# A mixture of experts on one core: quarter-row gathers issued one per unit of work instead of two

## The chip, the cores and the metric

The kernel runs on one core of a Trainium2 chip. The metric is device time in microseconds (us) of one execution, lower is better. The core has five engines that run at once, each with its own list of instructions in program order: TensorE (PE, matrix products), VectorE (DVE), ScalarE (ACT), GpSimd (POOL) and SyncE (SP, which here issues plain transfers). They wait for each other by semaphores.

## The reference

Attention for 8 batches of 8 heads (576 positions, head size 64) gives 4608 token rows of 512 numbers; then each token goes through one expert of eight, the one that its gate picks.

```python
logits = x @ w_gate                       # x: 4608 x 512, the attention's output
e_idx = np.argmax(logits, axis=1)
...
for e in range(E):                        # E = 8 experts, hidden size 1024
    mask = e_idx == e
    h = np.maximum(x[mask] @ w1[e], 0.0)
    ye = h @ w2[e]
    out[mask] = gate_w[mask, None] * eom[mask, e, None] * ye
```

## The kernel before

**Two phases.** The attention fills the first half of the time and stores each token's row (with its factors, 640 numbers) in DRAM as `xd`. The experts' phase works through 21 *slots*. A slot is up to 256 tokens of one expert ("pair"), or up to 128 ("single"); three pairs take up to 64 more tokens (three "long" slots, 9, 14 and 18). Slots 0 to 4 are pairs whose tokens are all known before the attention ends, and they gather whole rows. Slots 5 to 20 are the rest: 7, 10, 13, 16 and 19 are singles, the others pairs.

**A slot is eight units**, `j` = 0 to 7, written by `slot(s)`. Units 0 to 3 make the hidden layer: `first` puts 24 matmuls of a pair (12 of a single) into a PSUM tile `ph`, ACT takes the rectified result (`ht`, line 1417; 1400 in long slots), DVE the rest of it (line 1418 or 1401). There are two `ph` buffers, so the product of unit j+2 waits until ACT and DVE have emptied that of unit j. A single needs a further transpose on PE (`across`). Units 4 to 7 multiply by the second weights into `py` (line 1446). In each unit, ACT and DVE also split the weights of six units ahead into `wh` and `wl` (lines 1302, 1304; in singles, POOL makes two of eight `wl`), and SP loads those of eight units ahead. At unit 7 ACT and DVE write `y`, and POOL scatters it to `out` (line 1458; two or three scatters for a pair, one for a single).

**Gathers.** The rows of a later slot are fetched by POOL as indirect DMAs of 128 quarter rows each (line 1257, `part`): 8 for a pair, 4 for a single, 2 more for a long slot (`xgm`). They land in one of two buffers, `xg` of slot s modulo 2, so those of slot i can start once slot i-2 has been transposed out of it (`xr`, line 1320, and `gs`, line 1332, both on DVE). `gathers(s, j)` runs at the end of each unit: at unit 0 it puts the gathers of the next slots in the list `due`, and then issues up to a fixed number of them. All this only sets the *order* of POOL's list: POOL has no notion of a unit, and goes through gathers back to back until one of its instructions has to wait, which is a scatter (for `y`), a `wl` of a single's weights (for ACT's `wh`) or a gather into a buffer still in use. Where DVE transposes a slot's rows also follows from this bookkeeping: `turns` places the two transposes at units 6 and 7 of the slot two before, if the last gather was issued more than two units ago, and otherwise at units 2 and 3 of the slot before.

Of the kernel before, what the change touches and what calls it, by code (L numbers as in the profile page):

```python
# [870 lines left out]
class Moe:  # L871
# [390 lines left out]
    def gathers(self, s, j):  # L1262

        if j == 6 and s + 2 < self.end and self.whole(s + 2):
            self.gather(s + 2)
        if j == 0:
            for i in range(max(self.asked + 1, s + 2), min(s + 4, self.end)):
                if not self.whole(i):
                    self.due += [(i, b) for b in range(self.blocks(i))]
                    self.asked = i  # L1270
        for _ in range(2):
            if self.due:
                i, b = self.due[0]
                if (self.todo[i][1] if b < 8 else 3) in self.quarters and i - 2 in self.gss_made:
                    self.part(i, b)
                    self.due.pop(0)
                    if not any(g == i for g, _ in self.due):
                        self.asked_at[i] = 8 * s + j
# [329 lines left out]
```

## Time and profile before

| | us |
|---|---|
| median of 3 runs (lowest, highest) | 960.4 (959.22, 962.1) |
| the profiled execution: its own time | 968.01 |
| its span, first to last instruction | 966.2 |
| PE busy in the span | 899.8 (93%) |
| DVE busy | 769.8 (80%) |
| ACT busy | 640.3 (66%) |
| POOL busy | 621.3 (64%) |

The times of lines below are us from the start of the span of that one execution. "Busy" on PE counts its matmuls as the profile models them. An indirect DMA on POOL is shown for as long as POOL prepares it, not until its data lands.

### The profile page before, as it was taken

Reading aid. Unit: us, or ns where it says so; the run is one execution under the profiler, and the core shown is the slowest. Engines: PE = TensorE matmul, PEld = TensorE weight load, DVE = VectorE, ACT = ScalarE, POOL = GpSimd, SP = SyncE. Lnnn points to the kernel's source line nnn. Section 1 sums busy time; section 2 is a strip of 40 time slices with the busy share of each in tenths; the row PEclk is TensorE's granted clock in tenths of the full one; section 3 lists DMA queues with packets and bytes.
Section 4 is the critical chain, followed back from the end, with each engine's and each line's share of the span. In section 5 each row is a group of like instructions: output and inputs, shape, how many; then the busy total and the mean of one; then the engine's idle time right before and its main releaser. Section 6 shows DMA issues by size and latency. Waiting matters only on the chain.

```text
span 966.2 us, 33919 instructions
## 1 busy us (share of the span) xinstructions
PE 899.8 (93%) x14174; PEld 773.8 (80%) x14174; DVE 769.8 (80%) x1498; ACT 640.3 (66%) x1358; POOL 621.3 (64%) x560
## 2 busy tenths in 40 slices
PE   4999999999999999999999986999999998899997
PEld 3777777877878878887898975878979887788986
DVE  6899999999999999999597864859657587378661
ACT  4777788898989989886754533446537465265561
POOL 5788899898989899996221152678646664375310
PEclk9999999999999999999999997999999999999999
DMA  6365675665647565545699763768757677579530
GB/s 237 105 198 196 193 234 179 213 200 187 228 154 253 179 229 179 188 156 167 235 347 300 247 202 115 226 187 329 259 172 264 221 242 236 161 236 304 176 125 22
DMA packets 58624, 200.05 MB, mean 207 GB/s; under 512 B 8996, under 2 KB 11102, under 8 KB 58464
## 3 DMA queue, kind: packets, MB, share of 16 engines
q1 hardware_dynamic: 47616, 175.39, 55.1%
q0 software_dynamic: 9568, 21.27, 6.5%
q8 instruction: 113, 1.85, 0.8%
q10 hardware_dynamic: 1280, 1.15, 0.4%
q14 instruction: 47, 0.39, 0.1%
HBM read 177.21 MB, written 22.43 MB: 207 GB/s over the span
## 4 chain that ended last, share of the span: by engine, by line
PE 24%; issue 15%; POOL 7%; DVE 3%; another core or an unknown queue 2%; DMA 2%; ACT 1%; POOLq 0%; DVEq 0%; ACTq 0%
PE ph L1391 11%; PE py L1446 9%; POOL xg L1257 5%; DMA xg<-xd,1qi 2%; PE acc L612 1%; POOL out L1458 1%; DVE wl L1304 1%; POOL wl L1304 1%; PE py L1451 1%; PE ph L1377 1%; ACT wh L1302 1%; PE sc L566 0%; DVE pm L575 0%; DVE xr L1320 0%
## 5 line engine op out<-in xcount | busy, mean ns | idle before, releaser
L582 ACT ACTIVATE pm<-pm,m 128x576 f32<-128x576 f32 x288 | 222.0, 771 | 49.6 <-DVE pm L575 45.5
L1304 DVE TENSOR_TENSOR wl<-wr,wh 128x1024 fp32r<-128x1024 f32 x158 | 201.5, 1285 | 32.5 <-ACT wh L1302 25.6
L1391 PE MATMUL ph<-xt,wh 128*128 128x256 f32 (+1 forms) x1024 | 199.6, 293 | 24.2 <-issue 13.2
L575 DVE TENSOR_SCALAR_CACHE_REDUCE pm<-sc 128x576 f32<-128x576 f32 x288 | 205.3, 745 | 20.8 <-PE sc L566 14.4
L612 PE MATMUL acc<-pt,v 32*64 32x128 f32 (+1 forms) x9216 | 198.1, 295 | 13.8 <-DVE xb L641 7.7
L1446 PE MATMUL py<-wh,ht 128*128 128x512 f32 x592 | 194.3, 397 | 0.3 <-issue 0.2
L612 PEld LDWEIGHTS acc<-pt,v 32*64 32x64 f32 x9216 | 157.9, 131 | 39.1 <-issue 23.0
L1391 PEld LDWEIGHTS ph<-xt,wh 128*128 128x128 f32 x1024 | 165.0, 193 | 30.0 <-issue 15.6
L566 PE MATMUL sc<-kq 64*128 64x288 f32 x1536 | 162.3, 321 | 16.8 <-ACT kq L527 9.8
L1302 ACT CAST wh<-wr 128x1024 fp32r<-128x1024 f32 x168 | 171.4, 1049 | 0.0
L517 POOL TENSOR_TENSOR raw<-raw,rt 128x1152 f32<-128x1152 f32 x62 | 164.7, 2657 | 6.0 <-DMA raw<-in_qk 6.0
L566 PEld LDWEIGHTS sc<-kq 64*128 64x128 f32 x1536 | 122.8, 190 | 51.2 <-issue 21.2
L1391 PE MATMUL ph<-xt,wl 128*128 128x256 f32 (+1 forms) x512 | 149.4, 292 | 0.5 <-issue 0.5
L1257 POOL DMA_INDIRECT xg<-xd,2qi x88 | 104.9, 1192 | 45.5 <-issue 23.3
L1446 PEld LDWEIGHTS py<-wh,ht 128*128 128x128 f32 x592 | 111.3, 188 | 25.2 <-issue 1.1
L588 DVE STREAM_TRANSPOSE pt<-pm 128x576 f32<-128x576 f32 x160 | 116.7, 759 | 1.2 <-ACT pm L582 1.2
L1446 PE MATMUL py<-wl,ht 128*128 128x512 f32 x296 | 116.4, 393 | 0.7 <-issue 0.7
L1417 ACT ACTIVATE ht<-ph 128x512 fp32r<-128x512 f32 x52 | 31.1, 598 | 109.1 <-PE ph L1391 60.7
L1391 PEld LDWEIGHTS ph<-xt,wl 128*128 128x128 f32 x512 | 98.8, 193 | 0.9 <-issue 0.9
L1418 DVE SCALAR_TENSOR_TENSOR ht<-ph,ht 128x512 fp32r<-128x512 f32 x52 | 35.9, 690 | 70.9 <-ACT ht L1417 43.5
L590 DVE STREAM_TRANSPOSE pt<-pm 128x1152 f32<-128x1152 f32 x64 | 87.9, 1374 | 0.0
L530 POOL TENSOR_TENSOR kq<-raw,kq 128x1152 fp32r<-128x1152 f32 (+1 forms) x33 | 82.7, 2506 | 6.6 <-ACT kq L527 6.6
(308 smaller groups left out, 1159.7 us busy)
## 6 DMA issues: line engine op xcount, KB each, us to landing
wr<-in_w SPq DMA_DIRECT2D x168, 512.0 KB
raw<-in_qk SPq DMA_DIRECT2D x64, 576.0 KB
v<-in_v SPq DMA_DIRECT2D x64, 576.0 KB
xd<-xb SPq DMA_DIRECT2D x16, 640.0 KB
xg<-xd,2qi POOLq DMA_INDIRECT x88
xd<-xb SPq DMA_DIRECT2D x8, 160.0 KB
rt<-in_rope ACTq DMA_DIRECT2D x1, 576.0 KB
out<-y,2idx POOLq DMA_INDIRECT x22
```

The costliest lines, as they stand in the source:

```text
L517: self.eng(eng).tensor_tensor(out=rv, in0=rv, in1=rt, op=ALU.mult)
L566: self.sent.count(2, self.nc.tensor.matmul(self.ps[i][:, a, :HS], st, self.kq[r, mov, x], start=(n == 0), stop=(n == 2)))
L575: self.nc.vector.tensor_scalar(self.halves(i), self.ps[i][:, :, :HS], 1.0, FAR, op0=ALU.mult, op1=ALU.min, accum_out=self.m[i])
L582: self.nc.scalar.activation(self.pc[i], self.pc[i], AF.Exp, bias=self.m[i], scale=-1.0, accum_out=self.z[:, zi:zi + 1])
L588: self.nc.vector.transpose(out=self.pt[:, c + 5 * h, :], in_=self.pc[units[0]])
L590: self.nc.vector.transpose(out=self.pt[:, c:c + 6:5, :], in_=self.pc[units])
L612: m = nc.tensor.matmul(self.acc[h * D:h * D + D, a, o:o + 32 * n], self.v[r, h, j, :], self.pt[r, u:u + n, 32 * j:32 * j + 32], start=(j = ...
L1257: self.nc.gpsimd.indirect_dma_start(out=self.xgs[s % 2][:, b, :] if b < 8 else self.xgm[:, s % 2, b - 8, :], out_offset=None, in_=self.xd. ...
L1302: self.nc.scalar.copy(wh, r)
L1304: eng.tensor_tensor(out=wl, in0=r, in1=wh.bitcast(F32), op=ALU.subtract)
L1391: nc.tensor.matmul(out, st[:, dc, fs], mv[:, dc, 0:N], start=(n == 0), stop=(n == 11))
L1446: self.nc.tensor.matmul(py[h], st[:, f, hs], mv, start=(f == 0 and n == 0), stop=(f == 7 and n == 2))
```

## The change

In each unit, `gathers` issues one gather instead of up to two. It still issues two when the first one due is for the next slot (s+1) or earlier, or for a slot not above `n0` = 5, the first slot that is fetched by quarter rows.

```diff
-        for _ in range(2):
+        for _ in range(2 if self.due and self.due[0][0] <= max(s + 1, self.n0) else 1):
             if self.due:
                 i, b = self.due[0]
                 if (self.todo[i][1] if b < 8 else 3) in self.quarters and i - 2 in self.gss_made:
                     self.part(i, b)
                     self.due.pop(0)
```

No instruction is added or removed. On POOL the same gathers stand at other places between the scatters (`out`) and the `wl`. The first place is from the scatters of slot 5 to those of slot 8; before:

```order
L1458 DMA out_0<-y5_11634,2idx_10882 4608x512 x2
L1257 DMA xg_9170<-xd_83,2qi_10886 128x160 x6
L1304 TENSOR_TENSOR wl57_11799<-wr57_11724,wh57_11798 128x1024
L1257 DMA xg_9170<-xd_83,2qi_10886 128x160 x2
L1257 DMA xgm_11334<-xd_83,3qi_11608 128x160 x2
L1304 TENSOR_TENSOR wl61_11891<-wr61_11856,wh61_11890 128x1024
L1458 DMA out_0<-y6_11903,2idx_10882 4608x512 x2
L1257 DMA xg_9170<-xd_83,1qi_11281 128x160 x4
L1458 DMA out_0<-y7_12109,1idx_11277 4608x512
L1257 DMA xg_9170<-xd_83,2qi_10886 128x160 x8
L1458 DMA out_0<-y8_12370,2idx_10882 4608x512 x2
L1257 DMA xg_9170<-xd_83,2qi_10886 128x160 x6
```

and of the change, on the same engine and between the same scatters:

```order
L1458 DMA out_0<-y5_11619,2idx_10882 4608x512 x2
L1257 DMA xg_9170<-xd_83,2qi_10886 128x160 x4
L1304 TENSOR_TENSOR wl57_11778<-wr57_11709,wh57_11777 128x1024
L1257 DMA xg_9170<-xd_83,2qi_10886 128x160 x4
L1304 TENSOR_TENSOR wl61_11870<-wr61_11829,wh61_11869 128x1024
L1458 DMA out_0<-y6_11882,2idx_10882 4608x512 x2
L1257 DMA xg_9170<-xd_83,2qi_10886 128x160 x5
L1257 DMA xgm_11325<-xd_83,3qi_11593 128x160 x2
L1257 DMA xg_9170<-xd_83,1qi_11275 128x160
L1458 DMA out_0<-y7_12085,1idx_11271 4608x512
L1257 DMA xg_9170<-xd_83,1qi_11275 128x160 x3
L1257 DMA xg_9170<-xd_83,2qi_10886 128x160 x4
```

Behind a pair's scatters stand four gathers instead of six (slots 5 and 8), behind those of slot 6, where the single slot 7 begins, eight instead of four. The same pattern repeats for slots 8 to 17.

The second place is the start of POOL's quarter-row work. Before the scatters of slot 4 (`out` from y4) stood two gathers of slot 6, a gather of a list (`1tk`) and six more; in the change five follow `1tk`, and the rest goes behind the scatters:

```order
-L1257 DMA xg<-xd,2qi 128x160 x2
+L1257 DMA xg<-xd,2qi 128x160
 L955 DMA 1tk<-lst_85,1ri 11x128
-L1257 DMA xg<-xd,2qi 128x160 x6
-L1458 DMA out<-y_11311,0idx 4608x512 x2
-L1257 DMA xg<-xd,1qi 128x160 x2
+L1257 DMA xg<-xd,2qi 128x160 x5
+L1458 DMA out<-y_11305,0idx 4608x512 x2
+L1257 DMA xg<-xd,2qi 128x160
```

Two gathers of slot 6 have moved behind slot 4's scatters.

On DVE one thing moves: the transposes of slot 9 (`xr9`) and its factors (`gs9`), which stood before the first hidden part of slot 8 (`ht1_8`), now stand around the last one. Of the change:

```order
L1418 SCALAR_TENSOR_TENSOR ht1_8_12094<-ph8_2_12176,ht0_8_12093 128x512
L1304 TENSOR_TENSOR wl72_12204<-wr72_12135,wh72_12203 128x1024
L1320 STREAM_TRANSPOSE xr9_0_12209<-xg_9170 128x4x4x32
L1418 SCALAR_TENSOR_TENSOR ht1_8_12094<-ph8_3_12211,ht0_8_12093 128x512
L1304 TENSOR_TENSOR wl73_12239<-wr73_12171,wh73_12238 128x1024
L1320 STREAM_TRANSPOSE xr9_1_12244<-xg_9170 128x4x4x32
```

The lists of PE, ACT and SP are the same as before.

## Rows read from the trace of the kernel before

**Rows 1.** Stretches: length, busy PE, PEld, DVE, ACT, POOL; granted clock, DMA share, GB/s.

```profile
480.00:562.00 82.00, 81.71 (x523) 72.97 (x522) 69.18 (x183) 43.48 (x60) 13.68 (x12) 1.00 0.88 297
562.00:600.00 38.00, 26.01 (x140) 22.79 (x139) 16.72 (x39) 11.76 (x16) 19.78 (x20) 0.78 0.48 139
600.00:870.00 270.00, 256.69 (x1546) 228.59 (x1545) 187.17 (x290) 142.54 (x205) 161.24 (x124) 0.99 0.71 231
870.00:966.00 96.00, 89.61 (x541) 80.25 (x539) 56.58 (x79) 44.85 (x65) 26.34 (x20) 0.98 0.47 156
```

**Rows 2.** PE's time line: the matmuls before which it sat idle.

```profile
575.73 0.50 PE L1391 MATMUL ph<-xt,wh 128*128 128x256 f32 x2 [3.09 <-issue]
...
590.79 0.80 PE L1391 MATMUL ph<-xt,wh 128*128 128x256 f32 x2 [4.38 <-DVE ht L1418]
...
639.23 0.51 PE L1391 MATMUL ph<-xt,wh 128*128 128x256 f32 x2 [1.09 <-DVE ht L1418]
...
704.45 0.56 PE L1391 MATMUL ph<-xt,wh 128*128 128x320 f32 x2 [2.35 <-DVE ht L1401]
...
770.39 0.50 PE L1391 MATMUL ph<-xt,wh 128*128 128x256 f32 x2 [1.79 <-issue]
...
803.98 0.41 PE L1391 MATMUL ph<-xt,wh 128*128 128x320 f32 x1 [0.98 <-DVE ht L1401]
...
812.08 0.56 PE L1391 MATMUL ph<-xt,wh 128*128 128x320 f32 x2 [0.78 <-DVE ht L1401]
...
838.34 0.28 PE L1391 MATMUL ph<-xt,wl 128*128 128x256 f32 x1
...
844.77 0.50 PE L1391 MATMUL ph<-xt,wh 128*128 128x256 f32 x2 [3.31 <-issue]
```

**Rows 3.** ACT's time line: three late evictions of `ph`.

```profile
589.41 0.60 ACT L1417 ACTIVATE ht<-ph 128x512 fp32r<-128x512 f32 x1 [13.53 <-remote]
...
645.17 0.60 ACT L1417 ACTIVATE ht<-ph 128x512 fp32r<-128x512 f32 x1 [5.79 <-remote]
...
843.40 0.60 ACT L1417 ACTIVATE ht<-ph 128x512 fp32r<-128x512 f32 x1 [6.05 <-remote]
```

**Rows 4.** POOL's time line: last gathers of three runs, first behind wl57.

```profile
586.13 1.00 POOL L1257 DMA_INDIRECT xg<-xd,2qi  x1 [0.30 <-issue]
...
644.44 1.00 POOL L1257 DMA_INDIRECT xg<-xd,2qi  x1 [0.30 <-issue]
...
650.99 1.81 POOL L1257 DMA_INDIRECT xg<-xd,2qi  x1 [0.16 <-issue]
...
842.45 1.00 POOL L1257 DMA_INDIRECT xg<-xd,2qi  x1 [0.30 <-issue]
```

**Rows 5.** POOL's gathers grouped, in 561:588, then 724:758 (two groups), then 831:844.

```profile
L1257 POOL DMA_INDIRECT xg<-xd,2qi x16 | 16.2, 1015 | 16.8 <-PE mtp L1311 12.4 <-issue 4.1 <-remote 0.3
...
L1257 POOL DMA_INDIRECT xg<-xd,2qi x8 | 10.4, 1301 | 3.9 <-issue 1.8 <-DVE gs L1332 1.8 <-DVE ht L1418 0.3
L1257 POOL DMA_INDIRECT xg<-xd,1qi x4 | 6.2, 1541 | 1.2 <-issue 1.2
...
L1257 POOL DMA_INDIRECT xg<-xd,2qi x6 | 6.1, 1011 | 1.8 <-issue 1.8
```

**Rows 6.** Busy time in four shorter stretches with runs of gathers.

```profile
659.00:687.00 28.00, 27.23 (x176) 24.38 (x175) 25.79 (x38) 21.07 (x30) 21.63 (x16) 1.00 0.90 309
691.00:704.00 13.00, 11.09 (x74) 10.62 (x72) 5.18 (x8) 4.65 (x9) 8.69 (x8) 1.00 0.59 185
723.00:758.00 35.00, 35.00 (x226) 31.64 (x225) 28.23 (x40) 24.21 (x35) 23.16 (x18) 1.00 0.77 256
...
831.00:844.00 13.00, 10.46 (x81) 9.92 (x79) 2.67 (x3) 3.46 (x6) 9.10 (x9) 1.00 0.37 116
```

**Rows 7.** A gather's landing in the chain that ended last; DVE's transposes of slot 8.

```profile
733.60 5.40 DMA xg<-xd,1qi
...
654.72 1.29 DVE L1320 STREAM_TRANSPOSE xr<-xg 128x512 f32<-128x512 f32 x2
```

## The prediction

> **What bounds the kernel now.** I began with the busy time of each engine in long stretches, to see where PE, the busiest engine of the page, loses time. While the slots still gather whole rows, PE is busy 81.7 of 82 us; from 562 to 600 it is busy 26.0 of 38, at a mean granted clock of 0.78; from 600 to 870, 256.7 of 270 [rows 1]. So 25.3 us are lost between 562 and 870, which is about the time in which POOL issues quarter-row gathers. The 6.4 us after 870 are mostly the end of the program, where nothing else is left to do, and the change does not reach them.
>
> Second I read PE's time line for single gaps. Eight of them, 17.8 us together, stand before a product of the hidden layer [rows 2]. Such a product waits for the `ph` buffer, that is for ACT and DVE, so third I read ACT's line. ACT starts the eviction at 843.40 although PE ended that product at about 838.62 (the row at 838.34 plus 0.28), and nothing else occupies ACT [rows 2, 3]. What ended ACT's idle time is called remote: no finished instruction of the program explains it. PE's announcement of a finished product reached ACT late.
>
> Fourth I looked at what runs beside each late eviction. POOL is in an unbroken run of gathers and scatters, and three times ACT goes on about when that run ends: 843.40 against 843.45 (842.45 plus 1.00), 645.17 against 645.44, and 589.41 against 587.13, which is 2.3 us behind the end [rows 3, 4]. In these runs a gather takes 1.01 us and follows the last after 0.30 [rows 5]. That POOL's run holds back PE's announcement is my reading of the coincidence; the rows show no mechanism.
>
> It is not true of every run. From 723 to 758 POOL issues 14 gathers and 4 scatters with two short breaks, and PE is busy all 35 us; from 659 to 687 the loss is 0.8 of 28 us [rows 6]. There a gather takes 1.30 to 1.54 us [rows 5] and DVE is busy 81% and 92% of the time, against 40% and 21% in two stretches that stall [rows 6].
>
> **The change, part by part.** The rule counts gathers per unit, but POOL does not wait for units, so it does not pace anything. It only moves gathers across the scatters and `wl` at which POOL does wait. Its price is therefore in the length of the runs. One gather is 1.01 + 0.30 = 1.31 us of a fast run [rows 5].
>
> *Slot 4.* The run from 562 has 16 gathers, 2 scatters and a list gather, 19 in all [rows 5]; two gathers move behind the next scatters, 17 stay. If PE's release goes with the end of the run, it comes 2 x 1.31 = 2.6 us earlier, against the gap of 4.38.
>
> *Slots 6, 9, 12, 15 (the second pair after a single).* Behind the scatters stand four gathers in place of six; in slot 6 also, only three of slot 8's eight stay in front of the scatters, so a run of 16 falls into 3, a break, and 6. The end of the run comes 2.6 us earlier, which covers the gaps of 1.09, 2.35 and 1.79, and 2.6 of the 3.31 [rows 2].
>
> *Slot 14.* Seven gathers in place of eight: 1.3 of its 0.98 + 0.78.
>
> Sum of what is gained if the release follows the end: 2.6 + 1.1 + 2.35 + 1.8 + 2.6 + 1.3 = 11.75, say 11.7 us. The bound below is that the release does not move with the end at all: 0.
>
> *What the gathers land on.* Behind the scatters of slots 6, 9, 12 and 15, with which a single slot begins, stand eight or seven gathers in place of four, and these runs now go on without a break into the next pair. This order does not exist in the trace. The nearest rows are the stretches 659 to 687 and 723 to 758, which hold just these slots with 7 to 11 indirect DMAs a run: next to no loss [rows 6], so 0 is one bound. The other is the dearest gap of the trace behind a run of this kind, 3.31 us [rows 2], in each of the four: 13.2 us. I take 3, about a quarter, because the DVE there is busy and such runs have not stalled so far.
>
> *Later landing.* A gather lands up to 5.40 us after its start [rows 7]. The closest case is the last gather of slot 8, which now stands first behind `wl57`: started at 650.99, it would land at 656.4, and DVE wants it in the second of the two transposes at 654.72, at about 655.4 [rows 4, 7]. DVE waits about 1 us there, and I count a few such places (slots 10, 15 and 18 by the same counting). Behind DVE's wait stand `gs8`, the store of `y` and `wl` parts that PE uses some units later, so the cover is the six units by which weights are split ahead. I take 0; if that cover is gone, four waits of 1 us make 4.
>
> *The transposes of slot 9* move by eight units on DVE. They are then wanted at units 4 and 5 of slot 8 by `xt`, two units later. Their two halves of 0.65 us [rows 7], a short third one and the `gs` copies go from the busiest stretch of DVE to one with room. I take 0, with 1 either way inside the 3 above.
>
> *Weights.* Four gathers in place of two stand before `wl85` and `wl109`, so these are 2 x 1.84 = 3.7 us later (1.54 + 0.30 each) [rows 5]. They serve the sixth unit of the next slot, several units behind POOL's place. Cost 0.
>
> Sum against the profiled execution: 968.0 - 11.7 + 3 = 959.3 us. That execution is 7.6 us above the median of 960.4. I take the excess to be part of these stalls, since I see no other idle time of that size on PE, so that in the other runs (17.8 - 7.6) / 17.8 = 0.57 of them is left: 8.7 x 0.57 = 5.0, and 960.4 - 5.0 = 955.4. With the stalls whole in every run it would be 951.7.
>
> **The rivals.** *The release does not follow the end of the run.* Against the forecast speak the 2.3 us at 589.41, the release of slot 12, where PE goes on at 770.39, and the long runs that do not stall at all [rows 2, 6]. If the gaps come from something that the order of the gathers does not touch, or are in the main an effect of recording the trace (the excess of 7.6 us speaks for a part), the time is 960.4 and within 0.3% of it.
>
> *The singles stall instead.* A single's product is 12 matmuls, half of a pair's, so a late announcement has half the cover, and the transposes of `across` wait for the same eviction. If a run of ten holds PE's announcement there, the 13.2 us of the bound replace the 11.7 that is saved, less the share of it that stays anyway. With only half the saving in the other runs (5.9 x 0.57 = 3.3) and 13.2 x 0.57 = 7.5 lost, it is 960.4 + 4.2 = 964.6. It decides from two singles of four on, since 2 x 3.31 + 3 already outweighs most of 8.7.
>
> *POOL falls behind DVE.* In the stretches where the gathers go, a gather takes up to 1.54 us because DVE is busy [rows 5, 6]. Ten of them with 0.30 between take 18 us, 5 us more than at 1.31. The run then spills into the next pair, and slot 10's gathers land just when DVE transposes them. At 2 us each in three places, 6 of the 8.7 are eaten: 960.4 - 2.7 x 0.57 = 958.9, no change to be seen. The Trainium skill has a rule for this on the page "SBUF — State Buffer", section "SBUF: two separate sides": while VectorE runs an operation that takes both port pairs, GpSimd cannot write its descriptors, so a DMA of GpSimd waits for VectorE. The trace agrees in direction (1.01 against 1.30 to 1.54 us a gather), not in which operations do it.
>
> **How the numbers follow.** Runs that are shorter release PE earlier, net 951 to 957.5: 0.54. The release does not follow: 0.20. Singles stall: 0.18. POOL falls behind: 0.08. The predicted time is that of the first, 955.5. 0.3%, 2.9 us, is about what this measurement can tell from no change. The range is 948.5 (the whole 11.7, nothing lost) to 963 (into the rival with stalling singles), and leaves some 0.15 out; the likeliest case alone is 948.5 to 957.5. Faster is the first case with a sliver of the others, 0.56; same 0.25; slower the singles and a little of late landing, 0.19.
>
> **What the changed profile would show.** Right: from 562 to 870 PE loses clearly less than 25.3 us; the gaps in slots 9, 12 and 15 are below 1 us; ACT's late evictions end with POOL's shorter runs; slots 7, 10, 13 and 16 have no gap on PE, and DVE waits for landed gathers under 2 us a place. Wrong: gaps of the old size behind runs of four gathers (the release has another cause); gaps of 2 us and more in singles or at the start of slots 8, 11, 14 and 17; DVE transposes that wait 3 us and more; or gaps gone from the trace with the same median, which would mean that they belong to the recording.

## The result, and the profile after

The change takes 949.2 us (median of 20 runs, 944.4 to 959.6) against 960.5 (20 runs, 957.4 to 964.0) on the same chip: 0.988 of the time before, 95% interval 0.986 to 0.990, or 11.3 us less. The forecast was 5.0 us less. The profiled execution took 952.29 us, its span 950.5. Here and below, medians are of all runs, and intervals leave out runs more than 1.5% above the fastest of their kernel (in the second group nearly half of those of the kernel before).

The stretches of the trace after, with the columns of [rows 1]:

```profile
562.00:600.00 38.00, 31.49 (x164) 27.91 (x164) 22.58 (x55) 13.46 (x17) 19.28 (x18) 0.87 0.56 171
600.00:870.00 270.00, 263.31 (x1634) 236.94 (x1633) 197.31 (x297) 150.42 (x215) 174.11 (x133) 1.00 0.75 244
```

From 562 to 600 PE loses 6.5 us in place of 12.0, from 600 to 870 it loses 6.7 in place of 13.3: together 13.2 against 25.3 [rows 1]. PE's time line after, at the gaps that are left of [rows 2]:

```profile
575.01 0.50 PE L1391 MATMUL ph<-xt,wh 128*128 128x256 f32 x2 [2.46 <-issue]
583.73 0.80 PE L1391 MATMUL ph<-xt,wh 128*128 128x256 f32 x2 [4.05 <-issue]
757.17 0.51 PE L1391 MATMUL ph<-xt,wh 128*128 128x256 f32 x2 [1.00 <-DVE ht L1418]
789.68 0.56 PE L1391 MATMUL ph<-xt,wh 128*128 128x320 f32 x2 [1.38 <-DVE ht L1401]
797.60 0.56 PE L1391 MATMUL ph<-xt,wh 128*128 128x320 f32 x2 [0.60 <-DVE ht L1401]
828.90 0.51 PE L1391 MATMUL ph<-xt,wh 128*128 128x256 f32 x2 [1.81 <-DVE ht L1418]
```

The gaps of slots 6 and 9 (1.09 and 2.35 us in [rows 2]) are gone, those of slots 12 and 15 have shrunk (1.79 to 1.00, 3.31 to 1.81), those of slot 14 are as they were (0.98 + 0.78, now 1.38 + 0.60), and slot 4 still has its two. The eight gaps had 17.8 us together and now have 11.3: 6.5 of the 12.1 us by which PE loses less.

Nearly all of the rest, 5.5 us, are pauses of PE *inside* a product or between products, before matmuls that wait for no other engine. The trace before has 4.5 us of them in one product of slot 4, the trace after has none. Three of them, before:

```profile
581.51 0.37 PE L1391 MATMUL ph<-xt,wh 128*128 128x256 f32 x1 [1.05 <-issue]
582.96 0.37 PE L1391 MATMUL ph<-xt,wh 128*128 128x256 f32 x1 [1.08 <-issue]
585.09 0.37 PE L1391 MATMUL ph<-xt,wh 128*128 128x256 f32 x1 [1.04 <-issue]
```

That product lasted from 575.73 to 586.41, 10.7 us, where the first one of the slot took 3.0; the granted clock, 0.78 in the mean of the stretch, has a part in it. So beside the gathers not only PE's announcements are late, PE itself is held up.

ACT's late evictions in slot 4 after the change, and the end of POOL's run beside them:

```profile
582.36 0.60 ACT L1417 ACTIVATE ht<-ph 128x512 fp32r<-128x512 f32 x1 [7.19 <-remote]
586.76 0.60 ACT L1417 ACTIVATE ht<-ph 128x512 fp32r<-128x512 f32 x1 [2.88 <-remote]
```
```profile
584.12 1.89 POOL L1257 DMA_INDIRECT xg<-xd,2qi  x1 [0.30 <-issue]
```

ACT was released at 582.36, while POOL's run went on to 586.0: already here the release does not follow the end of the run.

### The profile page after: what moved, and what is told of

It is laid out like the page before. It is cut to its first block, busy times and chain, and to the rows that moved or that the text cites. A ratio compares the mean times of both kernels' runs of the same rounds, so it can differ in the third digit from the quotient of the medians.

```text
span 950.5 us, 33914 instructions
## 1 busy us (share of the span) xinstructions
PE 895.5 (94%) x14174; PEld 772.0 (81%) x14174; DVE 772.1 (81%) x1498; ACT 641.6 (68%) x1358; POOL 625.3 (66%) x560
## 4 chain that ended last, share of the span: by engine, by line
PE 42%; issue 7%; DVE 2%; ACT 1%; POOL 1%; DMA 1%; another core or an unknown queue 0%; POOLq 0%; DVEq 0%; ACTq 0%
PE py L1446 18%; PE ph L1391 18%; PE ph L1377 2%; PE py L1451 1%; PE acc L612 1%; POOL out L1458 1%; DMA xg<-xd,2qi 1%; PE sc L566 0%; DVE pm L575 0%; DVE wl L1304 0%; PE mtp L1311 0%; PE acc L628 0%; PE htp L1428 0%; ACT pm L582 0%
## 5 line engine op out<-in xcount | busy, mean ns | idle before, releaser
L1257 POOL DMA_INDIRECT xg<-xd,2qi x88 | 111.5, 1267 | 45.1 <-issue 25.2
L521 POOL TENSOR_TENSOR raw<-raw 128x1152 f32<-128x1152 f32 (+1 forms) x33 | 82.6, 2502 | 2.1
```

The costliest lines, as they stand in the source:

```text
L1257: self.nc.gpsimd.indirect_dma_start(out=self.xgs[s % 2][:, b, :] if b < 8 else self.xgm[:, s % 2, b - 8, :], out_offset=None, in_=self.xd. ...
```

## The experiments

The kernels ran in five groups, each group on one chip with the kernel before beside it. Those chips gave the kernel before 961.0, 953.9, 935.2, 954.6 and 952.3 us (medians), so a time is compared within its group only.

**First group: which part gains, and what the gathers cost (kernel before: 961.0 us).** The rule in slot 4 alone ("early"), or from slot 5 on alone ("late"):

```diff
-        for _ in range(2):
+        for _ in range(2 if s > 4 or self.due and self.due[0][0] <= max(s + 1, self.n0) else 1):   # early
+        for _ in range(2 if s < 5 or self.due and self.due[0][0] <= max(s + 1, self.n0) else 1):   # late
```

> One gather per unit in slot 4 only, two from slot 5 on: POOL's list is that of the change up to the scatters of slot 5 and that of the kernel before from there. My theory (a run of gathers holds PE's announcement back until about its end, so every shortened run gives its share): in the traces the change saved 5.5 us of PE's idle time between 562 and 600 and 6.6 us between 600 and 870, so this kernel should take 5 us off, about 955.5, and its trace should still show the gaps in slots 6, 9, 12 and 15. Rival, that slot 4 alone matters, because its gap also halves PE's clock: 949 to 951. Rival, that slot 4's gap is there only while a trace is recorded: 959.5 to 961.

> The other half: two gathers per unit in slot 4, one from slot 5 on. POOL's run from 562 is that of the kernel before, what follows the scatters of slot 5 is nearly the order of the change. My theory: the gaps of slot 4 stay at their old size (some 12 us of PE's idle time up to 600), those of slots 6 and 9 go, 960.5 - 6 = 954.5. Rival, that slot 4 alone matters: 959.5 to 961. Rival, that slot 4's gap is a thing of the recording: 949 to 951.

Measured: early 958.7, ratio 0.999 (0.996 to 1.002); late 951.5, ratio 0.989 (0.986 to 0.993). Most of the gain is in the later slots (9.5 us by the medians); early's 2.3 us are not clear of the noise. Windows of early (first two) and late:

```profile
562.00:600.00 38.00, 34.25 (x217) 31.64 (x216) 25.40 (x58) 15.40 (x20) 21.64 (x22) 0.91 0.68 204
600.00:870.00 270.00, 256.58 (x1552) 229.35 (x1551) 185.60 (x280) 143.92 (x206) 162.14 (x126) 0.99 0.71 235
```
```profile
562.00:600.00 38.00, 26.25 (x140) 22.38 (x138) 16.67 (x36) 11.55 (x15) 16.71 (x17) 0.78 0.49 149
600.00:870.00 270.00, 264.14 (x1634) 238.50 (x1634) 196.12 (x304) 148.24 (x213) 174.40 (x129) 0.99 0.75 243
```

Each trace shows its half mended (3.8 and 13.4 us lost in early, 11.8 and 5.9 in late, where the pauses inside a product of slot 4 are back, 4.3 us). But early's profiled run, 954.8 us, is the lowest of its 12 (up to 966.7): one trace of this program is a draw from a wide spread, and its time against the median says little.

Then the kernel before without gathers ("none"), and with a memset in place of each:

```diff
-                    self.part(i, b)
+                    self.nc.gpsimd.memset(self.xgs[i % 2][:, 0:6, :], 0.5)   # memset; left out in none
```

> The kernel before without any quarter-row gather from slot 5 on; scatters, list gathers and all other instructions stay in their order, and slots 5 to 20 multiply old rows. It gives the floor. My theory: with no runs left no eviction is late, PE idles no more than about 3 us between 562 and 870 in place of 25.3, and the time is 940 to 946. Rival, that the late evictions have nothing to do with the gathers: the gaps of 1 to 4 us stay, 955 to 961.

> The kernel before with each quarter-row gather replaced by a memset of 128 x 960 elements in the same buffer, which should keep POOL busy about as long (0.9 to 1.0 us) but moves nothing by DMA; slots 5 to 20 then multiply constants. My theory, that it is the indirect DMAs that hold PE's announcement back: as without gathers, 940 to 947. Rival, that a POOL that is busy without a break is enough (its instructions, its writes into SBUF beside DVE): the gaps stay and the time is 956 to 962.

Measured: 934.1 and 933.6 us, ratio 0.971 both (0.967 to 0.976). Windows of none, then of memset:

```profile
562.00:600.00 38.00, 38.00 (x254) 34.78 (x253) 30.77 (x72) 18.95 (x25) 8.03 (x9) 1.00 0.67 201
600.00:870.00 270.00, 267.29 (x1636) 240.78 (x1636) 204.31 (x298) 152.99 (x221) 46.57 (x32) 1.00 0.68 222
```
```profile
562.00:600.00 38.00, 38.00 (x258) 35.02 (x258) 31.31 (x68) 17.88 (x24) 21.47 (x25) 1.00 0.67 209
600.00:870.00 270.00, 267.29 (x1636) 240.98 (x1635) 202.07 (x298) 153.05 (x220) 129.78 (x126) 1.00 0.67 222
```

With a POOL that is busy for 21.5 of the 38 us, but with memsets, PE loses nothing up to 600, and neither trace has a matmul that pauses without a wait. So the gaps come from the gathers as DMAs, not from a busy POOL. And ordinary, unprofiled runs carry the whole loss: 961.0 - 934.1 = 26.9 us, about the 25.3 us of the trace [rows 1].

**Second group: length, pace, bytes, rows (kernel before: 953.9 us).** "unit" makes POOL wait for each unit, on top of the change (first two added lines); "spaced" keeps the order of the kernel before (last two):

```diff
+                    wh, _ = self.wp[min(8 * s + j + self.LEAD, 8 * self.end - 1)]     # unit
+                    self.mark(self.xgs[i % 2][0:1, b, 0:1] if b < 8 else self.xgm[0:1, i % 2, b - 8, 0:1], wh.bitcast(F32))
                     self.part(i, b)
+                    for _ in range(4):                                                # spaced
+                        self.nc.gpsimd.memset(self.pause, 0.5)
```

> The change, and ahead of each quarter-row gather a POOL copy of one element of the weights that ACT splits in that unit, written where the gather will land: POOL now really waits for the unit, so a run is no longer than one or two gathers (more only behind scatters). Theory of the run (what hurts is indirect DMAs back to back): nearly all of the 27 us that the gathers cost against the kernel without them come back, 936 to 943. Rival, that each gather costs PE its share wherever it stands: 946 to 952, as the change. Rival, that paced gathers land too late for the transposes: 955 and more, with DVE waiting for xg.

> The kernel before, its order untouched, with four memsets of 128 x 128 (some 0.8 to 1.0 us on POOL) behind every quarter-row gather. A gather then starts every 2.2 us or so and a run takes 1.7 times as long. Theory as I predicted by it (PE's announcement is held until the end of the run): the stalls grow with the run, 965 to 980. Rival, the pace (the announcement is held only while indirect DMAs follow each other at 1.3 us): the stalls go, 938 to 948. Rival, each gather costs the same wherever it stands: 957 to 963.

unit took 941.9 us (0.993, 0.989 to 0.997; by the medians 0.987). In its trace no eviction waits for an announcement that nothing explains (remote); the one large gap, 4.8 us, is another wait, of DVE for rows that landed late, which holds the hidden layer behind it:

```profile
783.47 0.71 DVE L1322 STREAM_TRANSPOSE xr<-xg 128x512 f32<-128x512 f32 x1 [3.70 <-DMA xg<-xd,2qi]
```

The 941.9 us lie in the range that the theory gave, but the chip is another one: the ratio is that of the change on its own chip (0.988). The change did not run in this group.

spaced took 1005.8 us (1.059, 1.053 to 1.065). The sign is that of the theory of the run's end, the reason is not. PE's waits there, with their line, sum, number and longest:

```profile
PE ph L1380 <- POOL wl L1307: 24.1, 2, 12.4
PE 1tr L969 <- DVE 1tk L964: 9.2, 1, 9.2
PE py L1449 <- POOL wl L1307: 9.1, 3, 3.9
PE 3tr L969 <- DVE 3tk L964: 8.8, 1, 8.8
```

POOL is late with what it does besides: the `wl` of singles and the lists that PE transposes. ACT's evictions are on time in slot 4, in the middle of a run of gathers that now takes longer:

```profile
574.15 0.60 ACT L1420 ACTIVATE ht<-ph 128x512 fp32r<-128x512 f32 x1 [1.32 <-PE ph L1394]
577.00 0.60 ACT L1420 ACTIVATE ht<-ph 128x512 fp32r<-128x512 f32 x1 [1.32 <-PE ph L1394]
```

So the theory by which I predicted, that PE is held until about the end of the run, falls. Half the bytes or half the rows of each gather:

```diff
-            out=self.xgs[s % 2][:, b, :] if b < 8 else ..., in_=... x=BW)[0:n, :]
+            out=self.xgs[s % 2][:, b, 0:BW // 2] if b < 8 else ..., in_=... x=BW // 2)[0:n, :]   # halfbytes
+            out=self.xgs[s % 2][0:64, b, :] if b < 8 else ..., (ids[0:64])                       # halfrows
```

> The kernel before with quarter-row gathers of 80 of the 160 numbers of each row: as many rows, half the bytes; the other half of each buffer keeps old numbers, so the output is not the reference's. If the bytes that the gathers move are what holds PE's announcement: half of the 27 us come back, 945 to 950. If it is the indirect DMA as POOL prepares it (a row is a row), the time stays at 957 to 963.

> The kernel before with each quarter-row gather fetching 64 rows in place of 128: half the rows and half the bytes in as many gathers; the other half of the buffer keeps old rows, so the output is not the reference's. If the work of preparing rows is the cause: a gather takes about 0.5 us less on POOL and 945 to 950 results, or less where the stalls die out altogether (938). If it is the number of indirect DMAs, whatever they hold: 957 to 963.

halfbytes: 947.5 us, 0.995 (0.990 to 0.999); halfrows: 959.9 us, 1.013 (1.004 to 1.022). The one is a little better, the other no better, though both move the same number of bytes. With 64 rows a gather still occupies POOL for 0.94 us, and the late evictions are there, here with 5.6 us of idle ACT ahead of one:

```profile
585.68 0.60 ACT L1417 ACTIVATE ht<-ph 128x512 fp32r<-128x512 f32 x1 [5.63 <-remote]
```

Fewer rows in a gather do not help; whether bytes have a part stays open.

**Third group: a chip without the gaps (kernel before: 935.2 us).** The change again; "unit2" is the copies of unit with the old rule; "pause1" is the change with one memset of 128 x 128 behind each gather; "four" is the old rule with `range(4)`.

```diff
                     self.part(i, b)
+                    self.nc.gpsimd.memset(self.pause, 0.5)     # pause1
```

> The change itself again, for the comparisons of this call on one chip. By its first timing 0.988 of the kernel before; on a chip on which the kernel before stalls less, the gain should be smaller in proportion.

> The kernel before with its rule of two gathers per unit, and ahead of each gather the POOL copy of an element of the weights that ACT splits in that unit. POOL really waits for units, but gets two gathers in each, earlier than with the rule of the change. Pace theory (what hurts are indirect DMAs at 1.3 us one behind the other; two and a copy are no such run): no late announcement, and no wait for landing rows either, 936 to 942, at least as fast as one per unit with the same copies (941.9 against 953.9 of the kernel before). Rival, that the number of gathers per unit matters as such: like the kernel before, or at most half of the gain of the change.

> The change with one memset of 128 x 128 (0.2 us and its issue) behind every gather, so that gathers start every 1.6 to 1.7 us in place of 1.3 in a run, near the 1.6 to 1.84 us of the stretches that never stalled. Pace theory: the late announcements that the change left go, 3 to 8 us faster than the change, less what POOL loses by being later (wl of the singles). Theory of the end of the run: 0 to 5 us slower than the change.

> The kernel before with up to four gathers per unit: behind the scatters of slots 5, 8, 12 and 15 stand eight in place of six (of slots 5 and 15 ten with those of xgm), the singles keep four. This is the step of my prediction turned round: each such run ends 2.6 us later (5.2 in two places), so if the length of a fast run sets the stall, 10 to 15 us slower than the kernel before. Rival, that length does not matter: within 3 us of the kernel before.

Measured: the change 933.7 (0.998, 0.996 to 1.000); pause1 936.0 (1.000, 0.999 to 1.002); unit2 948.5 (1.013, 1.011 to 1.015); four 944.6 (1.009, 1.006 to 1.012). Here the kernel before takes about what the kernel without gathers took on the first group's chip (934.1), and little is left to gain. The trace of the change shows why, first its window and then ACT beside a run of gathers 1.31 us apart:

```profile
562.00:600.00 38.00, 38.00 (x259) 35.04 (x258) 31.03 (x66) 18.22 (x24) 26.33 (x27) 1.00 0.82 245
```
```profile
573.04 0.60 ACT L1417 ACTIVATE ht<-ph 128x512 fp32r<-128x512 f32 x1 [1.31 <-PE ph L1391]
575.88 0.60 ACT L1417 ACTIVATE ht<-ph 128x512 fp32r<-128x512 f32 x1 [1.31 <-PE ph L1391]
```

Program and order are those of the change on the first chip, where ACT stood idle for 7.19 us at this place; here it waits 1.31 us for the next product and no more. four loses 9.4 us, near the 10 to 15 expected, but no eviction in its trace ends on remote; longer runs there delay the lists:

```profile
PE 1tr L969 <- DVE 1tk L964: 4.4, 1, 4.4
PE 3tr L969 <- DVE 3tk L964: 2.5, 1, 2.5
```

unit2 loses 13.3 us by such waits too (3.2 us for `3tk`, 4.8 for `wl` of POOL), against my expectation of a gain.

**Fourth group: the kernel before traced again (954.6 us).**

> The kernel before itself, for its trace on the chip of this call. If the late evictions are what separates the chips: PE's idle time between 562 and 870 follows the time of the kernel, some 3 to 5 us where it takes 935 us and some 25 us where it takes 960. If the chips differ in something else: 25 us of idle time at any time.

> The change. If it only takes away part of these stalls: 0.988 of the kernel before where that takes 960 us, 0.998 where that takes 935 us.

> The change with a POOL copy ahead of each gather that waits for the unit's weights. Pace theory: on a chip that stalls no eviction is late, 940 to 944 and 5 to 9 us faster than the change; what is left are waits for rows that land late. On a chip that does not stall these waits are all that shows: 3 to 10 us slower than the change.

> The change with a memset of 0.2 us behind each gather. Pace theory: on a chip that stalls, 2 to 6 us faster than the change; on a chip that does not, 0 to 3 us slower (by its first run 936.0 against 933.7). Theory of the number in a row: the same as the change on both, or slower.

Measured: the kernel before itself 953.1 (1.000, 0.998 to 1.003); the change 945.4 (0.991, 0.988 to 0.995); unit 943.7 (0.991, 0.987 to 0.994), 1.7 us below the change where 5 to 9 were expected (what is left are DVE's waits for late rows, 7.2 us in three waits); pause1 936.4 (0.983, 0.979 to 0.987), clearly faster than the change. Windows of the kernel before, of the change, and of pause1:

```profile
562.00:600.00 38.00, 32.08 (x189) 28.60 (x188) 22.46 (x54) 13.64 (x18) 19.28 (x19) 0.91 0.63 183
600.00:870.00 270.00, 263.27 (x1612) 235.39 (x1611) 196.60 (x293) 152.29 (x218) 173.83 (x132) 1.00 0.75 245
```
```profile
562.00:600.00 38.00, 31.98 (x180) 28.26 (x179) 22.93 (x57) 13.82 (x18) 19.59 (x19) 0.91 0.57 171
600.00:870.00 270.00, 266.62 (x1646) 240.28 (x1646) 204.15 (x307) 153.87 (x219) 178.50 (x133) 1.00 0.77 251
```
```profile
562.00:600.00 38.00, 37.59 (x238) 33.64 (x237) 31.82 (x85) 17.84 (x24) 25.55 (x35) 1.00 0.76 229
600.00:870.00 270.00, 266.61 (x1637) 239.96 (x1636) 202.68 (x299) 153.09 (x219) 193.30 (x233) 1.00 0.77 252
```

PE's idle time from 562 to 870 in the kernel before goes with the time of the run: 25.3 us in a run of 968.0 us on the first chip, 12.7 in one of 948.0 here (the lowest of 12). On the chip of 935.2 us the kernel before was not traced. Slot 4 loses 6 us with the change as without it; with pause1 it loses 0.4. And this is POOL in slot 4 in pause1:

```profile
577.78 1.02 POOL L1258 DMA_INDIRECT xg<-xd,2qi  x1 [0.16 <-issue]
578.80 0.22 POOL L1277 MEMSET pause<- 128x128 f32 x1
579.18 1.01 POOL L1258 DMA_INDIRECT xg<-xd,2qi  x1 [0.17 <-issue]
```

A gather follows the last after 1.40 us in place of 1.31, in a run that is as long as before. My second theory, that the pace holds PE's announcement, expected 1.6 to 1.7 us. 0.09 us more is hardly another pace, but no kernel sets gathers 1.40 us apart without an instruction between them, so the pace is not ruled out. ACT in that run, of the change and then of pause1:

```profile
580.33 0.60 ACT L1417 ACTIVATE ht<-ph 128x512 fp32r<-128x512 f32 x1 [7.11 <-remote]
```
```profile
579.38 0.60 ACT L1419 ACTIVATE ht<-ph 128x512 fp32r<-128x512 f32 x1 [1.32 <-PE ph L1393]
583.57 0.60 ACT L1419 ACTIVATE ht<-ph 128x512 fp32r<-128x512 f32 x1 [2.66 <-PE ph L1393]
```

Not all lateness is gone: the eviction at 583.57 comes after 2.66 us where 1.32 is normal. But none of 7 us is left.

**Fifth group: memset or memory (952.3 us).** "tile_only" is the change with the small tile of pause1 set aside and one memset of it at the start; "pause_before" is pause1 with the old rule `range(2)`.

> The change with the 512 bytes per partition of the pause tile set aside and one memset of it at the start, none behind gathers. If the layout of memory was what helped pause1: like pause1_c, 0.983 of the kernel before on a chip where that takes 953 us or more. If the memset between gathers was: like the change, 0.988 to 0.992. On a chip where the kernel before takes 935 us the two can't be told apart.

> The kernel before, with its rule of two gathers per unit and its order, and one memset of 128 x 128 behind each gather. If the memset between gathers takes the late evictions away by itself: 0.980 to 0.988 on a chip that stalls, no late evictions in the trace, and the rule of the change adds little beside it. If the number of gathers in a row is what counts: 0.995 to 1.005, the late evictions of slots 4, 6, 9, 12 and 15 still there. POOL is later by 0.1 us a gather, so that wl and the list gathers of slots 4 and 5 may cost 1 to 3 us.

Measured: tile_only 945.0 (0.993, 0.989 to 0.997), like the change; pause_before 938.0 (0.985, 0.983 to 0.988), like pause1. Windows of tile_only, then of pause_before:

```profile
562.00:600.00 38.00, 37.35 (x253) 34.20 (x253) 29.77 (x65) 17.14 (x23) 30.20 (x25) 1.00 0.76 242
600.00:870.00 270.00, 263.13 (x1582) 236.05 (x1581) 197.01 (x292) 149.53 (x214) 167.72 (x127) 0.99 0.74 244
```
```profile
562.00:600.00 38.00, 37.92 (x259) 34.90 (x258) 30.86 (x71) 17.77 (x23) 33.46 (x45) 1.00 0.76 237
600.00:870.00 270.00, 264.81 (x1609) 237.15 (x1608) 199.20 (x296) 151.77 (x217) 189.32 (x225) 1.00 0.74 248
```

The two traces differ little (0.65 and 0.08 us lost up to 600, 6.9 and 5.2 after), so this reading rests on the times. It is the memset between two gathers that helps, not the layout of memory, and it needs no change of the order. But it does not take every late eviction away, as was expected. In pause_before one is late in slot 6, beside the two scatters of slot 5, behind which no memset stands, and one each in slots 12 and 15, beside gathers that do have their memsets (749.97 and 817.97). PE, however, has no gap before a product there:

```profile
619.27 0.60 ACT L1419 ACTIVATE ht<-ph 128x512 fp32r<-128x512 f32 x1 [2.84 <-remote]
749.97 0.60 ACT L1419 ACTIVATE ht<-ph 128x512 fp32r<-128x512 f32 x1 [4.24 <-PE ph L1393]
817.97 0.60 ACT L1419 ACTIVATE ht<-ph 128x512 fp32r<-128x512 f32 x1 [4.31 <-PE ph L1393]
```

On the chips that show the gaps, pause1 and pause_before gave 0.983 and 0.985 where the change gave 0.991 (fourth group) and its near copy 0.993 (fifth).

## Why the prediction was right in direction and wrong in size

- **The loss and its place.** Right in the main. PE waits for `ph` because ACT's eviction starts late, and the gathers are behind it: without them PE loses nothing from 562 to 600 and 2.7 us from 600 to 870. But I explained 17.8 of the 25.3 us, and overlooked that PE also pauses where it waits for no engine (5.5 us).
- **The sum of the gains, 11.7 us.** Close as a whole, on the first chip, and by luck: the trace lost 12.1 us less of PE's time, the timed runs 11.3. The eight gaps of which I made the sum gave 6.5 of the 12.1; the other 5.5 came from the pauses, which I had not priced. In slot 4 I had 2.6 us off the gap of 4.38, which stayed at 4.05. I had 9.1 us in slots 6 to 15, and late, which has the later slots alone, gained 9.5 in timed runs; but the trace of the change gains 6.6 from 600 to 870, slot 14's 1.3 did not come, and slots 12 and 15 kept 1.0 and 1.8. In timed runs slot 4's part is not shown: early's interval reaches from 3.8 us faster to 2.3 slower.
- **The share of 0.57: the step that failed.** I took the 7.6 us by which the profiled run exceeded the median for stalls that the other runs lack, and scaled all gains by it. The timed runs have them in full: 26.9 us over the kernel without gathers. The excess was one draw of a spread that reaches 22 us on one chip (940.7 to 962.9).
- **The 3 us for long runs in singles: the other step.** Nothing was lost there. After the change PE is busy through the singles (slots 7, 10, 13 and 16):

```profile
646.00:658.00 12.00, 12.00 (x81) 10.92 (x80) 11.70 (x16) 10.37 (x18) 10.21 (x7) 1.00 0.82 272
712.00:724.00 12.00, 12.00 (x81) 10.92 (x80) 8.40 (x11) 10.55 (x18) 9.87 (x8) 1.00 0.61 190
771.00:783.00 12.00, 12.00 (x81) 10.97 (x80) 11.59 (x16) 10.36 (x19) 9.54 (x6) 1.00 0.90 288
843.00:855.00 12.00, 12.00 (x81) 10.94 (x80) 9.48 (x13) 10.37 (x19) 10.30 (x7) 1.00 0.88 283
```

  With neither term the sum gives 960.4 - 11.7 = 948.7, where 949.2 was measured; 8.7 unscaled, 951.7. So these two terms account for the size, on top of a sum whose parts were off both ways.
- **Later landing, at nothing.** Right: DVE waits 1.6 us for landing rows in two waits, the longer 1.3, where I counted about 1 us a place under cover.
- **That the release goes with the end of the run.** Wrong as the mechanism. spaced, pause1 and pause_before have runs as long or longer and no such lateness in slot 4. In slot 15 the eviction came after 4.63 us of idle ACT in the trace of the change, with four gathers behind the scatters, and after 4.53 in that of the kernel before on the fourth group's chip, with six (first and second line):

```profile
827.53 0.60 ACT L1417 ACTIVATE ht<-ph 128x512 fp32r<-128x512 f32 x1 [4.63 <-PE ph L1391]
823.44 0.60 ACT L1417 ACTIVATE ht<-ph 128x512 fp32r<-128x512 f32 x1 [4.53 <-PE ph L1391]
```

  What most of the late evictions need is gathers 1.31 us apart with nothing between. The change breaks such rows up: behind a pair's scatters four, then a wait for ACT's `wh`, in place of six. That it gains by this is my reading of the traces.
- **The rivals.** That the release does not follow the run's end is true of the mechanism, but not what I concluded from it, no change. The singles did not stall. POOL does get slower beside DVE, as the third rival has it (a gather of a pair takes 1.27 us on the mean, before 1.19), with no gap on PE that shows a cost.
- **What I did not foresee**: the gain depends on the chip. 11.3 us on the first, 9.2 on that of the fourth group, 1.5 on that of the third, where "the same" would have been the right answer.

What holds PE's announcement back, physically, stays open. That it takes indirect DMAs of POOL in quick succession, on some chips, is shown, and that a memset between two of them takes most of the loss away; why the memset helps, and which path the DMAs share with PE, is not. Two other causes the trace before speaks against. Lack of instructions: from 577 to 592 no packet of the instruction queues moved, yet ACT went on at 589.41 and PE at 590.79. Sheer traffic: 139 GB/s from 562 to 600, against 297 just before, where PE lost 0.3 of 82 us [rows 1].

## What to carry to other kernels

When a wait ends for no reason that the trace shows, take the suspected neighbour out and time the floor: two short kernels (no gathers, memsets for gathers) told here what the whole effect was worth and in which runs. Don't scale a sum by how one profiled run stands to the median unless the spread of the runs is known. Where POOL issues many small indirect DMAs beside a busy PE, try a short POOL instruction between them before reordering anything: it cost 0.09 us a gather and gained 18 us with the new order and 14 with the old one, where the change and its near copy gained 9 and 7 on the same chips, and pause1 lost nothing to speak of (1.000) where there was nothing to gain.

## What the runs showed of the hardware that I had not expected

- The same program takes 935 us on one chip and 952 to 961 on others. What differs in the traces of the change are the late evictions beside gathers: after up to 7.2 us of idle ACT on two chips, none on that one. Without gathers the kernel before took 934 us on a chip where it takes 961 with them.
- Beside a run of such gathers PE can also pause before matmuls that wait for no engine (1.04 to 1.08 us, three times in one product). Not every trace has it: 4.5 and 4.3 us in slot 4 on the first two chips, 0.3 in that of the kernel before on the fourth group's chip.
- An indirect DMA of 64 rows occupies POOL nearly as long as one of 128: 0.94 against 1.00 us.
- A memset of 0.22 us between two gathers shortens the time before the next from 0.30 to 0.16 us, so that the pair costs 1.40 us in place of 1.31.
